# Pooled attention in an attention and two-MoE kernel: maxima scaled by ScalarE, a third batch's weights normalised there, and a re-planned order of issue

## The chip, the cores and the metric

The kernel runs on one core of a Trainium2 chip. The metric is the device time of one execution in microseconds (us). Before the change it is 820.82 us, the median of three runs (820.48 to 821.06).

## What is computed

Local and pooled attention over four batches, then two feed-forward layers in succession (2304 tokens, 512 to 2048 to 512), cut from the reference:

```python
q_d = q.reshape(B, H, Sd, factor, D).mean(axis=3)      # k_d and v_d likewise; factor 4
out_d = sm_attn(q_d, k_d, v_d)                          # softmax attention, 144 x 144 per head
out_up = np.repeat(out_d, factor, axis=2)
mask = np.abs(pos[:, None] - pos[None, :]) < factor
out_local = np.matmul(softmax(where(mask, scores, -1e9)), v)
x = (out_up + out_local)                                # B 4, H 8, S 576, D 64
h = x @ w_in;  g = np.maximum(0.01 * h, h);  x = g @ w_out          # layer 1
h = x @ w_in2; g = where(h >= 1, h, where(h <= -1, 0, (h + 1) ** 2 / 4)); out = g @ w_out2   # layer 2
```

## The kernel before

**A list of operations and a planner.** The kernel first makes a list of some thousands of operations (`Op`: an engine, a planned duration, the function that issues its instructions, the operations it depends on, a due time `key`). `Issue.run` then plays the list through in planned time: whenever an engine is free, the ready operation with the smallest rank on it is taken and its function called, so that its instructions stand next in the engine's queue. The order of every queue, and which buffer and PSUM bank an operation gets, come out of this. The numbers at the head of the file (due-time offsets per chain in `DUE`, leads, windows, latencies) steer it. The instructions' own semaphore waits are put in afterwards by the framework, from the data that they share.

**The operations of attention** stand in chains, one per pair of heads:

- `prep` loads q, k and v of batches 0 and 1 and transposes q and k on TensorE (L1185; its copies out of PSUM are ScalarE's, L1209).
- `down` is the pooled attention of one batch and head pair, four batches by four pairs. VectorE finds the row maxima (`peak`, L1367, two calls each for two heads by two row halves) and multiplies them by minus the softmax scale (L1368); ScalarE takes exponentials with that as bias (`pexp`, L1375); VectorE makes the reciprocal of the sums (L574, L575); then the weights are normalised (`norm`): by ScalarE in four calls where the batch is in `NORM_ACT_D` (L1388), otherwise by one VectorE multiplication (L1392).
- `local_p` and `local_d` are the local attention, on TensorE for batches 0 and 1 and most of it on VectorE for the rest (L1705 to L1779).

**Weights of the first layer** are converted to float32 by VectorE in three steps and split into two float16 parts, high by ScalarE and low by VectorE (first pairs: L701, L707, L713, L727, L729; in the second layer's stages L852 to L877). Every product of the two layers is three float16 matmuls.

**The layers.** Layer 1 is tiled into blocks of 512, 512, 512, 512 and 256 tokens: `g1` (L1934) makes a bank of hidden values by twelve matmuls, `g2` (L2196) multiplies it by the output weights. Layer 2 uses a seven-product scheme for both of its products: L1964 for the first, L2133 for the second, with the sums and splits in between on VectorE and ScalarE (L1995 to L2103). At a block's end its last sums go through `onto` (L2154) and a store (L2165).

**Fills.** Where the planner sees TensorE idle for want of work, up to the planned time `FILL`, it issues a matmul of zeros into a spare bank (`fill`, L2529). These stand in TensorE's queue like any other work.

The two functions of `down` that change read, before:

```python
nc.vector.reduce_max(ml(0, par), psv(par), axis=AX)               # peak, L1367
nc.vector.tensor_scalar_mul(ml(0, par), ml(0, par), -s_e)         # peak, L1368
...
nc.scalar.activation(out=p[:, par, a, :], in_=psv(par)[:, a, :], func=AF.Exp, scale=s_e,
                     bias=ml(0, par)[:, a:a + 1], accum_out=ml(1, par)[:, a:a + 1])   # pexp, L1375
```

Of the kernel before, what the change touches and what calls it, by code (L numbers as in the profile page):

```python
# [27 lines left out]
LEAD_O = 2  # L28
WINDOW_O = 15
OUT_GAP = 0.411  # L30
LAG7 = {0: 10, 1: 9, 2: 15, 3: 18, 4: 10}
G2LATE = {0: 7.366, 1: 6.364, 2: 4.968, 3: 5.548, 4: 9.226}
PASS2 = {0: 47.587, 1: 3.15, 2: 56.047, 3: 70.737, 4: 41.965}
SOON = 1000.0
FP = 2
T4_LATE = 12
EARLY_O = 4
W1_SPARE = 1957
LATE1 = 5.273
# [4 lines left out]
WINDOW_T = 7  # L44
# [5 lines left out]
WINDOW_A = 19  # L50
WINDOW_D = 15
LEAD_W = 6
LEAD_W1 = 1.5
LEAD_W1O = 1.477
RUSH_B = {1: 7.782}
RUSH_P = None
W1_RUSH = 0
QUEUE = 2.793
# [3 lines left out]
WINDOW_B = {2: 6, 3: 6}  # L62
LEAD_D = 2
# [4 lines left out]
DMA_END = 1.377  # L68
SW_END = 2.263
# [6 lines left out]
RUN_PE = 0.06  # L76
# [6 lines left out]
D_PE = 24.191  # L83
D_STRETCH = 1.006
W1_FROM = 9
W1_MORE = 1.467
# [10 lines left out]
PEAK_D = 4921  # L97
RESERVE = 3947
HP_GAP = 0.8
RESERVE_W = 0  # L100
SPARE = 5950

TWO_FROM = (2, 98)
WINDOW = 22
WINDOW_W = 34
LIMIT = 26744
AHEAD = 5
LEAD_Q = (12, 8)
O_LATE = 1.34
LAGMAX = 5  # L110
G2KEY = 1.87

NORM_ACT = (1,)
NORM_ACT_D = (1,)
FILL = 173.83


DUE = {0: -0.12, 2: 0.03, 3: -0.01, 9: 2.8, 10: -0.4, 14: -3.31, 17: -9.75, 19: -0.21,
# [129 lines left out]
class Issue:  # L248
# [4 lines left out]
    SHAPE = 0.093  # L253

# [36 lines left out]
    def run(self, fill=None):  # L291
# [16 lines left out]
        while left:  # L308
# [94 lines left out]
class Banks:  # L403
# [13 lines left out]
    def get(self, for_mlp=False):  # L417
        self.mlp += for_mlp
        self.begun |= for_mlp
        return self.free.pop(0)  # L420

# [6 lines left out]
def kernel(  # L428
# [85 lines left out]
    T_SC = 0.553  # L514
# [222 lines left out]
    class Pair:  # L737


        def __init__(self, n, nu):  # L740
# [3 lines left out]
            self.ready = []  # L744

# [382 lines left out]
    def prep(b, hp, due):  # L1128
# [93 lines left out]
        for nm in "qk":  # L1222
            c = None
            for i in range(2):
                n = (NA, QBB - NA)[i]
                t = ch.op("PE", pe_mm(RUN_PE * 2 * n, QB, 2 * n, D) if b in RUNS else pe_tr(QB, n, QB), lambda nm=nm, i=i: tr(nm, i), [ld[nm]], banks=1, shape=(1, 1) if b in RUNS else (2, 2),
# [12 lines left out]
    def down(b, hp, due):  # L1239
# [238 lines left out]
    def local_p(b, n0, cnt, hp, due):  # L1478
# [152 lines left out]
        x1[blk].ready.append(o)  # L1631
        ch.close()
# [10 lines left out]
    def local_d(u, due):  # L1643
# [201 lines left out]
        for par in range(2):  # L1845
# [16 lines left out]
            o = ch.op("DVE", 0.36 + 0.16 * sum((r == 0) + (r + n == SEGB) for _, n, _, r in rr),  # L1862
# [7 lines left out]
        for jh, j0 in enumerate(range(0, L, JC)):  # L1870
            last = []
            for par in (1, 0) if (0, j0) in v_act else (0, 1):
# [25 lines left out]
                ch.op("DVE", t_dve(512), lambda jh=jh: xl(jh), [h], after=freer(("x", jh))))  # L1898
        ch.close()
# [13 lines left out]
    def stage(m, b):  # L1913
# [8 lines left out]
        def g1(p, i):  # L1922
# [646 lines left out]
```

## Time and profile before

| | |
|---|---|
| median of the runs | 820.82 us |
| the profiled execution, its own time | 821.11 us |
| its span, first to last instruction | 819.3 us |
| TensorE busy | 812.0 us, 99%, 6791 matmuls |
| VectorE busy | 726.5 us, 89%, 1360 instructions |
| ScalarE busy | 499.1 us, 61%, 1283 instructions |
| granted TensorE clock, mean | 1.000 |

The profiled execution took 821.11 us, of which 1.81 us lie around its span. An engine's busy time is the time in which it had an instruction under way; matmuls overlap, so a busy TensorE may still be doing fills, or matmuls shorter than the time they are shown with. In the rows below PE is TensorE's matmuls, PEld its weight loads, DVE is VectorE, ACT ScalarE, POOL GpSimd and SP the queue that issues most transfers.

### The profile page before, as it was taken

The numbers are of one execution on the slowest core, as the hardware profiler recorded it, in microseconds if no ns is written. First come the engines' busy times: TensorE is split into PE (matmuls) and PEld (weight loads), VectorE is DVE, ScalarE is ACT, GpSimd is POOL, SyncE is SP. The second block draws the span as 40 slices with busy tenths as digits, with TensorE's granted clock in tenths as the row PEclk, the third lists the DMA queues.
The fourth block names the chain that finished last, engine by engine and source line by source line (L and its number), as shares of the span: only waits on it lengthen the run. The fifth ranks groups of instructions, "written<-read, shape, count | busy, mean of one in ns | idle before, by whom it ended". The sixth has DMA issues, their size and how long they took to land. (4 is left out here: it accounts for less than half of the span.)

```text
span 819.3 us, 17419 instructions
## 1 busy us (share of the span) xinstructions
PE 812.0 (99%) x6791; PEld 562.6 (69%) x6791; DVE 726.5 (89%) x1360; ACT 499.1 (61%) x1283; POOL 38.7 (5%) x60
## 2 busy tenths in 40 slices
PE   9999999999999999999999999999999999999997
PEld 6765554544454444544446888888888888889986
DVE  4999999999999999999999999999669697896761
ACT  4987667466436463473356677777567676775640
POOL 1010000033001310000000000000000000000000
PEclk9999999999999999999999999999999999999999
DMA  8877556576345822331733320010000200100001
GB/s 207 207 193 232 190 187 172 155 145 126 92 124 168 134 44 69 100 103 55 253 103 129 110 73 27 2 52 27 26 2 14 78 14 2 52 27 2 3 27 52
DMA packets 63521, 77.40 MB, mean 94 GB/s; under 512 B 17742, under 2 KB 41678, under 8 KB 63438
## 3 DMA queue, kind: packets, MB, share of 16 engines
q1 hardware_dynamic: 52238, 72.13, 28.4%
q0 software_dynamic: 11200, 4.15, 4.5%
q8 instruction: 53, 0.87, 0.4%
q14 instruction: 30, 0.25, 0.1%
HBM read 66.80 MB, written 9.44 MB: 93 GB/s over the span
## 5 line engine op out<-in xcount | busy, mean ns | idle before, releaser
L1934 PE MATMUL bank<-arena,w 128*128 128x512 f16 (+1 forms) x960 | 197.0, 358 | 0.0
L2196 PE MATMUL bank<-arena,w 128*128 128x512 f16 x768 | 176.4, 379 | 0.3 <-DVE arena L2176 0.3
L1934 PEld LDWEIGHTS <-w 128*128 128x128 f16 x960 | 92.5, 98 | 88.9 <-issue 1.9
L2196 PEld LDWEIGHTS <-w 128*128 128x128 f16 x960 | 92.0, 98 | 86.9 <-issue 2.3
L2133 PEld LDWEIGHTS <-w 128*128 128x128 f16 x1086 | 106.0, 98 | 12.2
L2133 PE MATMUL bank<-arena,w 128*128 128x256 f16 x810 | 96.8, 273 | 0.0
L1964 PEld LDWEIGHTS <-w 128*128 128x128 f16 x960 | 86.4, 98 | 10.0 <-issue 1.3
L2046 ACT ACTIVATE arena<-bank 128x512 f32<-128x512 f32 x64 | 38.0, 593 | 81.5 <-PE bank L1934 79.2
L2050 ACT ACTIVATE w<-bank,half 128x512 f32<-128x512 f32 x66 | 45.3, 687 | 41.5 <-DVE bank L2013 38.8
L1964 PEld LDWEIGHTS <-arena 128*128 128x128 f16 x720 | 64.8, 98 | 6.7
L2099 ACT ACTIVATE w<-w 128x256 f16<-128x256 f32 (+1 forms) x112 | 50.2, 478 | 17.4 <-DVE w L2058 13.2
L1964 PE MATMUL bank<-arena,w 128*128 128x256 f16 (+1 forms) x480 | 59.9, 267 | 0.6 <-DVE bank L2006 0.4
L2058 DVE SCALAR_TENSOR_TENSOR w<-w,bank 128x512 f32<-128x512 f32 x66 | 44.8, 681 | 15.0 <-ACT w L2054 14.0
L2103 DVE SCALAR_TENSOR_TENSOR w<-w 128x256 f16<-128x256 f32 (+1 forms) x112 | 53.1, 502 | 3.6 <-ACT w L2099 3.5
L1964 PE MATMUL bank<-w,w 128*128 128x256 f16 (+1 forms) x480 | 52.6, 256 | 0.0
L1995 ACT COPY w<-bank 128x256 f32<-128x256 f32 x106 | 36.4, 365 | 18.2 <-PE bank L1964 16.5
L2133 PEld LDWEIGHTS <-arena 128*128 128x128 f16 x426 | 41.6, 98 | 5.5 <-issue 0.7
L1964 PE MATMUL bank<-arena 128*128 128x256 f16 (+1 forms) x384 | 44.6, 266 | 0.0
L2176 DVE SCALAR_TENSOR_TENSOR arena<-arena 128x512 f16<-128x512 f32 x64 | 43.6, 682 | 0.3 <-ACT arena L2172 0.3
L1779 DVE TENSOR_TENSOR arena<-arena 128x768 f32<-128x768 f32 (+2 forms) x60 | 41.1, 687 | 1.4
L2054 ACT ACTIVATE w<-w 128x512 f32<-128x512 f32 x66 | 41.1, 628 | 1.2
L2172 ACT ACTIVATE arena<-arena 128x512 f16<-128x512 f32 x64 | 40.3, 630 | 0.9
(219 smaller groups left out, 1342.0 us busy)
## 6 DMA issues: line engine op xcount, KB each, us to landing
arena<-in_moe_w_in_dram SPq DMA_DIRECT2D x15, 1024.0 KB
arena<-in_moe_w_out_dram SPq DMA_DIRECT2D x8, 1024.0 KB
arena<-in_moe_w_out_dram SPq DMA_DIRECT2D x9, 512.0 KB
arena<-x SPq DMA_DIRECT2D x4, 1024.0 KB
x<-arena SPq DMA_DIRECT2D x15, 256.0 KB
w<-in_moe_w_out_dram SPq DMA_DIRECT2D x7, 512.0 KB
out_dram<-w SPq DMA_DIRECT2D x14, 256.0 KB
arena<-in_k_dram SPq DMA_DIRECT2D x23, 112.0 KB
```

The costliest lines, as they stand in the source:

```text
L1779: nc.vector.tensor_tensor(out, x, y, op=ALU.add)
L1934: nc.tensor.matmul(h[:, e], a[:, f // FP, c, f % FP], y[:, :, c, :], start=(n == 0), stop=(n == 3 * KDM - 1),)
L1964: nc.tensor.matmul(o[:, e], a[:, i, c], y[:, k, c, :], start=first and e == 0 and n == 0, stop=n == 5, skip_group_check=True,)
L2050: nc.scalar.activation(out=t, in_=st["h", p], func=AF.Relu, scale=0.5 * s_in, bias=half)
L2054: nc.scalar.activation(out=t, in_=t, func=AF.Square, scale=s_in ** -0.5)
L2058: nc.vector.scalar_tensor_tensor(out=t, in0=t, scalar=1.0 / s_in, in1=st["h", p], op0=ALU.min, op1=ALU.max)
L2099: nc.scalar.activation(out=left(p, part, q0, q1)[:, 0], in_=src(), func=AF.Copy, scale=so)
L2103: nc.vector.scalar_tensor_tensor(out=d[:, 1], in0=src(), scalar=so, in1=d[:, 0], op0=ALU.mult, op1=ALU.subtract)
L2133: nc.tensor.matmul(o[:, k], a[:, i, at:at + P], y[:, j], start=opens and p == e == k == n == 0, stop=p == PH - 1 and e == E - 1 and n == 2 ...
L2172: nc.scalar.activation(out=gv(p)[0], in_=st["t", p].ap, func=AF.Copy, scale=so)
L2176: nc.vector.scalar_tensor_tensor(out=lo, in0=st["t", p].ap, scalar=so, in1=hi, op0=ALU.mult, op1=ALU.subtract)
L2196: nc.tensor.matmul(o, a, y[:, e, :], start=(first and n == 0 and c % E == 0), stop=(last and n == 2), skip_group_check=True,)
```

## The change

- `peak` finds the negated maxima in one instruction; the multiplication by the scale moves from VectorE to ScalarE, at the head of `pexp`.
- `NORM_ACT_D` takes in batch 2, so that its pooled weights are normalised by ScalarE, four calls for each of four head pairs, in place of one VectorE multiplication each.
- The planner no longer adds an engine's hop (0.15 to 0.25 us of planned time) between two operations of the same engine.
- Many of the planner's numbers are others, among them `FILL`, `DUE`, `PASS2`, `G2LATE`, `LAG7` and several planned durations. Code for splitting the first `g1` by heads is added, but `EARLY = 0` leaves it unused.

```diff
-LAG7 = {0: 10, 1: 9, 2: 15, 3: 18, 4: 10}
-PASS2 = {0: 47.587, 1: 3.15, 2: 56.047, 3: 70.737, 4: 41.965}
+LAG7 = {0: 8, 1: 13, 2: 14, 3: 16, 4: 6}
+PASS2 = {0: 36.519231, 1: 8.162466, 2: 62.712205, 3: 115.505985, 4: 38.456233}
+EARLY = 0
...
-NORM_ACT_D = (1,)
-FILL = 173.83
+NORM_ACT_D = (1, 2)
+FILL = 60
...
-DUE = {0: -0.12, 2: 0.03, 3: -0.01, 9: 2.8, 10: -0.4, 14: -3.31, 17: -9.75, 19: -0.21,
...
+DUE = {0: -0.01, 2: -0.15, 4: 5.57, 5: -1.03, 6: -0.01, 7: -0.11, 9: 8.0, 10: -0.27, 12: -0.05,
...
-                    u.ready = max(u.ready, d + self.HOP[op.eng]
-                                  + (self.HOP_PE if u.eng == "PE" else 0.0))
+                    hop = 0.0 if u.eng == op.eng and not op.lat else (
+                        self.HOP[op.eng] + (self.HOP_PE if u.eng == "PE" else 0.0))
+                    u.ready = max(u.ready, d + hop)
...
-            nc.vector.reduce_max(ml(0, par), psv(par), axis=AX)
-            nc.vector.tensor_scalar_mul(ml(0, par), ml(0, par), -s_e)
+            nc.vector.reduce_max(ml(0, par), psv(par), axis=AX, negate=True)
...
             p = st["p"].ap[:GH].rearrange("p (h a g) -> p h a g", h=2, a=2)
+            nc.scalar.mul(ml(0, par), ml(0, par), s_e)
             for a in range(2):
                 nc.scalar.activation(
...
-            e = ch.op("DVE", 0.56, lambda par=par: peak(par), [o, e], need=() if par else (8,))
-            x = ch.op("ACT", 2 * t_act(G, True, 2), lambda par=par: pexp(par), [e, x],
+            e = ch.op("DVE", t_dve(2 * G), lambda par=par: peak(par), [o, e], need=() if par else (8,))
+            x = ch.op("ACT", 2 * t_act(G, True, 2) + 0.1, lambda par=par: pexp(par), [e, x],
```

What it makes of the queues is shown at three places. Lines of the changed kernel have other numbers: L1185 is there L1196, L1367 L1378, L1375 L1386, L1934 L1951, L2133 L2150, L2154 L2171, L2165 L2182 and L2529 L2554; its new L1384 is the scaling on ScalarE.

VectorE, early in batch 0's pooled attention, before:

```order
L1287 TENSOR_REDUCE w_61<-w_61 128x144
L1367 TENSOR_REDUCE w_61<-bank_69 72x2
L1368 TENSOR_SCALAR w_61<-w_61 72x2
L1278 TENSOR_TENSOR arena<-arena 72x4x128
L1280 TENSOR_TENSOR w_61<-arena 72x2x2x64
L1367 TENSOR_REDUCE w_61<-bank_64 72x2
L1368 TENSOR_SCALAR w_61<-w_61 72x2
```

ScalarE at the same chain, in the changed kernel:

```order
L1384 ACTIVATE w_61<-w_61 72x2
L1386 ACTIVATE arena,w_61<-bank_69,w_61 72x144 x2
L1568 COPY arena<-bank_65 70x512
L1384 ACTIVATE w_61<-w_61 72x2
L1386 ACTIVATE arena,w_61<-bank_70,w_61 72x144 x2
```

The 72x2 multiplications are gone from VectorE's queue and stand on ScalarE's, each right ahead of the two exponentials that use it; there are 32 of them.

TensorE just ahead of layer 1's first `g1`, before:

```order
L1512 MATMUL bank_66<-w_61,arena 64x70 x6
L1185 MATMUL bank_64<-ident,arena 64x64 x8
L2529 LDWEIGHTS zeros
L2529 MATMUL bank_63<-zeros 128x512
...
L1353 MATMUL bank_67<-w_61 72x144
L1353 MATMUL bank_69<-w_61 72x144
L1353 MATMUL bank_67<-w_61 72x144
L1353 MATMUL bank_69<-w_61 72x144
L1934 LDWEIGHTS w_79
L1934 MATMUL bank_68<-arena,w_79 128x512
```

and in the changed kernel:

```order
L1196 MATMUL bank_64<-ident,w_61 64x64 x10
L2554 LDWEIGHTS zeros
L2554 MATMUL bank_63<-zeros 128x512
L1564 MATMUL bank_65<-ident,w_61 70x128 x4
L1196 MATMUL bank_69<-ident,w_61 64x64 x8
L1196 MATMUL bank_68<-ident,w_61 64x64 x8
L1364 MATMUL bank_70<-w_61 72x144
...
L2554 LDWEIGHTS zeros
L2554 MATMUL bank_63<-zeros 128x512
L1951 LDWEIGHTS w_79
L1951 MATMUL bank_66<-arena,w_79 128x512
```

The real matmuls ahead of the first `g1` are the same but for batch 1's transposes (L1185, 216 before, 252 now). Of the fills 40 stood ahead of it and 11 behind; now 43 stand ahead and none behind. What the first `g1` needs of VectorE is its first 144 instructions before and 141 now: eight L1368 less, and more by one local maximum (L1525) and the four instructions of a third weight tile of 128x512 (L701 to L729). Of ScalarE it needs 121 before and 136 now, eight of the new ones being L1384.

VectorE at the program's end, before:

```order
L2154 SCALAR_TENSOR_TENSOR w_79<-bank_67,w_79 128x256
L2154 SCALAR_TENSOR_TENSOR w_79<-bank_63,w_79 128x256
L2154 SCALAR_TENSOR_TENSOR w_79<-bank_64,w_79 128x512
L2154 SCALAR_TENSOR_TENSOR w_79<-bank_70,w_79 128x512
```

and in the changed kernel:

```order
L2171 SCALAR_TENSOR_TENSOR w_79<-bank_67,w_79 128x256
L2171 SCALAR_TENSOR_TENSOR w_79<-bank_65,w_79 128x512
L2171 SCALAR_TENSOR_TENSOR w_79<-bank_63,w_79 128x256
L2171 SCALAR_TENSOR_TENSOR w_79<-bank_67,w_79 128x256
```

The last sum and the store behind it are now those of the block of 256 tokens, half as wide (128x256, 128 KB in place of 256 KB).

## Rows read from the trace of the kernel before

**Rows 1.** The page, busy time, share of the span, instructions.
```profile
PE 812.0 (99%) x6791; PEld 562.6 (69%) x6791; DVE 726.5 (89%) x1360; ACT 499.1 (61%) x1283; POOL 38.7 (5%) x60
```

**Rows 2.** The page, granted TensorE clock in 40 slices, tenths of full speed.
```profile
PEclk9999999999999999999999999999999999999999
```

**Rows 3.** Four stages by windows: us, busy us (instructions) by engine, clock, DMA share, GB/s.
```profile
0.00:20.00 20.00, 18.80 (x288) 11.93 (x290) 9.69 (x32) 9.39 (x34) 3.81 (x22) 1.00 0.80 206
20.00:58.00 38.00, 38.00 (x662) 28.55 (x660) 35.48 (x116) 33.64 (x149) 4.24 (x7) 1.00 0.79 207
58.00:120.00 62.00, 62.00 (x544) 33.14 (x543) 60.17 (x116) 45.45 (x143) 1.58 (x5) 1.00 0.65 205
120.00:440.00 320.00, 319.62 (x1741) 154.48 (x1739) 314.98 (x470) 166.47 (x454) 29.03 (x26) 1.00 0.46 122
```

**Rows 4.** The chain that ended last, last part: start, us, what.
```profile
798.28 0.43 DVE w L2154
...
798.75 15.89 PE bank L2133 x144
...
814.67 0.69 DVE w L2154
```

**Rows 5.** Windows of L2529 alone (fills): us, PE busy (count), PEld busy (count).
```profile
0.00:58.00 58.00, 15.43 (x40) 3.86 (x40) 1.00 0.80 207
58.00:120.00 62.00, 3.41 (x11) 0.91 (x11) 1.00 0.65 205
```

**Rows 6.** PE's waits from 58 us on: us in total, times, longest.
```profile
PE bank L2133 <- DVE w L2154: 0.5, 1, 0.5
PE bank L1964 <- DVE bank L2006: 0.4, 1, 0.4
PE bank L2196 <- DVE arena L2176: 0.3, 1, 0.3
PE bank L1964 <- DVE bank L2013: 0.2, 1, 0.2
```

**Rows 7.** Groups by line: count, busy us, mean ns, idle before.
```profile
L1368 DVE TENSOR_SCALAR w<-w 72x2 f32<-72x2 f32 x16 | 2.7, 166 | 0.6
...
L1392 DVE TENSOR_TENSOR arena<-arena 72x576 f32<-72x576 f32 x8 | 6.0, 748 | 0.0
...
L1388 ACT ACTIVATE w<-w 72x144 f32<-72x144 f32 x8 | 2.7, 408 | 1.7 <-DVE w L575 1.7
...
L1864 ACT ACTIVATE arena<-arena 128x56 f32<-128x56 f32 x10 | 2.5, 251 | 10.8 <-DVE arena L1734 10.8
...
L1375 ACT ACTIVATION_READ_ACCUMULATOR arena<-bank,arena 72x1 f32 x32 | 6.3, 197 | 0.0
```

**Rows 8.** Windows of L1368 alone: us, DVE busy (count).
```profile
0.00:120.00 120.00, 1.99 (x12) 1.00 0.72 206
```

**Rows 9.** Timeline, 0 to 14 us: start, us, engine, line, what.
```profile
1.20 4.02 PE L2529 MATMUL bank<-zeros 128*128 128x512 bf16 x9 [1.20 <-DVE half L533]
...
7.16 1.73 PE L1185 MATMUL bank<-ident,w 64*64 64x64 f32 x52
```

**Rows 10.** Timeline, around 93 us.
```profile
91.08 0.68 DVE L713 SCALAR_TENSOR_TENSOR w<-arena,w 128x512 int32<-128x512 int32 x1
...
92.02 1.22 DVE L729 SCALAR_TENSOR_TENSOR w<-arena,w 128x1024 f16<-128x1024 f32 x1
...
93.30 0.82 PE L2529 MATMUL bank<-zeros 128*128 128x512 bf16 x3
...
93.96 0.81 PE L1934 MATMUL bank<-arena,w 128*128 128x512 f16 x3
```

**Rows 11.** Timeline, the end.
```profile
802.88 0.42 DVE L2154 SCALAR_TENSOR_TENSOR w<-bank,w 128x256 f32<-128x256 f32 x1 [4.18 <-PE bank L2133]
...
815.39 0.38 SPq L2165 DMA_DIRECT2D out_dram<-w  x1
```

More of the change, by code (lines that the diff above doesn't have):

```diff
@@ L27 @@
 OUT7 = (0,1,2,3,4)
-LEAD_O = 2
-WINDOW_O = 15
-OUT_GAP = 0.411
-LAG7 = {0: 10, 1: 9, 2: 15, 3: 18, 4: 10}
-G2LATE = {0: 7.366, 1: 6.364, 2: 4.968, 3: 5.548, 4: 9.226}
-PASS2 = {0: 47.587, 1: 3.15, 2: 56.047, 3: 70.737, 4: 41.965}
+LEAD_O = 5
+WINDOW_O = 30
+OUT_GAP = 0.369438
+LAG7 = {0: 8, 1: 13, 2: 14, 3: 16, 4: 6}
+G2LATE = {0: 12.156149, 1: 14.308722, 2: 2.469313, 3: 8.213399, 4: 16.039018}
+PASS2 = {0: 36.519231, 1: 8.162466, 2: 62.712205, 3: 115.505985, 4: 38.456233}
 SOON = 1000.0
 FP = 2
-T4_LATE = 12
+EARLY = 0
+EARLY_ROOM = 0
+T4_LATE = 8.301867
 EARLY_O = 4
-W1_SPARE = 1957
-LATE1 = 5.273
+W1_SPARE = 3131
+LATE1 = 8.859782
 LEAD_S = 4
@@ L43 @@
 LEAD_T = 4
-WINDOW_T = 7
+WINDOW_T = 8
 LEAD = 5
@@ L49 @@
 RUSH = 1.0e4
-WINDOW_A = 19
-WINDOW_D = 15
+WINDOW_A = 17
+WINDOW_D = 22
 LEAD_W = 6
-LEAD_W1 = 1.5
-LEAD_W1O = 1.477
-RUSH_B = {1: 7.782}
+LEAD_W1 = 1.06903
+LEAD_W1O = 2.28811
+RUSH_B = {1: 7.935746}
 RUSH_P = None
 W1_RUSH = 0
-QUEUE = 2.793
+QUEUE = 2.381903
 WHOLE = ()
@@ L61 @@
 POOLED = ()
-WINDOW_B = {2: 6, 3: 6}
-LEAD_D = 2
+WINDOW_B = {2: 7, 3: 6}
+LEAD_D = 1
 D_GAP = 4
@@ L67 @@
 DMA_LAST = 0.85
-DMA_END = 1.377
-SW_END = 2.263
+DMA_END = 1.710062
+SW_END = 0.8
 SW_FIRST = 1.88
@@ L82 @@
 LAT_W = (1.95, 1.95)
[L83 to L86, printed above, removed]
+D_PE = 80
+D_STRETCH = 0.871542
+W1_FROM = 10
+W1_MORE = 1.749148
 D_ACT = (0,1)
@@ L96 @@
 ADD_PE = ()
-PEAK_D = 4921
-RESERVE = 3947
-HP_GAP = 0.8
+PEAK_D = 5347
+RESERVE = 2527
+HP_GAP = 0.695866
 RESERVE_W = 0
-SPARE = 5950
+SPARE = 5857
 TWO_FROM = (2, 98)
[L104 to L111, printed above, removed]
-NORM_ACT = (1,)
-NORM_ACT_D = (1,)
-FILL = 173.83
-DUE = {0: -0.12, 2: 0.03, 3: -0.01, 9: 2.8, 10: -0.4, 14: -3.31, 17: -9.75, 19: -0.21,
[7 rows of a table removed]
+WINDOW = 24
+WINDOW_W = 29
+LIMIT = 26359
+AHEAD = 4
+LEAD_Q = (10, 8)
+O_LATE = 4.133946
+LAGMAX = 7
+G2KEY = 1.232175
+NORM_ACT = (1,)
+NORM_ACT_D = (1, 2)
+FILL = 60
+DUE = {0: -0.01, 2: -0.15, 4: 5.57, 5: -1.03, 6: -0.01, 7: -0.11, 9: 8.0, 10: -0.27, 12: -0.05,
[9 rows of a table added]
 class Arena:
@@ L420, in get, with hold @@
         return self.free.pop(0)
+    def hold(self):
+        self.mlp += 1
+        return self.get()
     def put(self, t, for_mlp=False):
@@ L744, in __init__ @@
             self.ready = []
+            self.by = {c: [] for c in range(KDM)}
         def make(self):
@@ L1861, in local_d @@
                 reds.append(o)
-            o = ch.op("DVE", 0.36 + 0.16 * sum((r == 0) + (r + n == SEGB) for _, n, _, r in rr),
+            o = ch.op("DVE", 0.36 + 0.32 * sum((r == 0) + (r + n == SEGB) for _, n, _, r in rr),
                       lambda par=par: soft1(par), reds, need=(L,))
@@ L1898, in local_d @@
                 ch.op("DVE", t_dve(512), lambda jh=jh: xl(jh), [h], after=freer(("x", jh))))
+            for by in x1[blk].by.values():
+                by.append(ch.ops[-1])
         ch.close()
@@ L1920, in stage, with g1 @@
         x = x1[b] if m == 1 else None
-        def g1(p, i):
-            sch.step = max(sch.step, i)
-            h_open[0] += 1
+        def g1(p, i, cs=range(KDM)):
+            if KDM - 1 in cs:
+                sch.step = max(sch.step, i)
+                banks.begun = True
             hi, lo = x[0], x[1]
             whi, wlo = w_in[m]
-            st["h", p] = banks.get(True)
+            if 0 in cs:
+                h_open[0] += 1
+                st["h", p] = banks.hold()
             h = st["h", p].rearrange("p (a u n) -> p a u n", a=E, n=x.nu)
@@ L1930, in g1 @@
                 f = E * p + e
-                n = 0
-                for c in range(KDM):
+                n = 3 * cs[0]
+                for c in cs:
                     for a, y in ((whi, hi), (whi, lo), (wlo, hi)):
@@ L2269, in stage @@
             fs = [E * p + e for e in range(E)]
-            o1 = sch.add(
+            o1 = None
+            if m == 1 and not b and p < EARLY:
+                for c in range(KDM):
+                    o1 = sch.add(
+                        "PE", 3 * t_mm(N) * E, lambda p=p, i=i, c=c: g1(p, i, (c,)),
+                        x.by[c] + [o1] + [w_ready[m, 0, f] for f in fs], key=float(i),
+                        banks=0 if c else 1, mlp=True, cols=3 * 512,
+                        gate=None if c else (lambda: len(banks.free) > EARLY_ROOM))
+            o1 = o1 or sch.add(
                 "PE", 12 * t_mm(N) * E, lambda p=p, i=i: g1(p, i),
```

8 lines of the change are left out of this document (5 added, 3 removed), and 16 rows, old and new, of the table DUE.

## The prediction

> **What bounds the kernel now.** I read the page's busy times first. TensorE is busy for 99% of the span and VectorE for 89% [rows 1]. Both cannot be the bound everywhere, so I then read the same by stages [rows 3]. Up to 20 us every engine waits for the first loads and for the others. From 20 to 440 us VectorE works almost without a break: 35.48 of 38 us, 60.17 of 62, 314.98 of 320. TensorE shows as full there too, but part of what it does is multiplying zeros: 40 fills with 15.43 us of busy time up to 58 us, where the first `g1` starts, and 11 with 3.41 us between 58 and 120 us [rows 5]. Behind 120 us there are no fills, and TensorE's waits on VectorE from 58 us to the end come to four, 1.4 us in all [rows 6]. The chain that ended last shows the rest: TensorE, broken by VectorE for 0.43 us at 798 us, and a last VectorE sum of 0.69 us [rows 4].
>
> So TensorE's real work is the floor, and this change takes none of it away. What can be won is the time in which TensorE has no real work: the fills, the 1.4 us of waits, and the 4.6 us behind its last matmul. Everything behind 58 us comes to 3.4 + 1.4 us and a piece of the tail. That caps the gain however much VectorE is relieved.
>
> **The change, part by part.**
>
> *VectorE's relief.* 32 multiplications by the scale go, at 0.166 us [rows 7]: 5.3 us. Four of the normalisations go (batch 2, one for each head pair), at 0.748 us [rows 7]: 3.0 us. Together 8.3 us of 726.5. The negated maximum takes the place of the plain one, same shape, and I cost that at nothing. All of this lies in the stages that VectorE fills, yet only 12 of the scalings, 2.0 us, fall before 120 us [rows 8], and the normalisations of batch 2 come later. Behind 120 us there are only waits to win. So 6.3 of the 8.3 us meet a TensorE that hardly waits.
>
> *ScalarE's load.* 32 scalings of 72x2: the trace has none. The nearest rows are 0.197 us (reading an accumulator, one element) and 0.251 us (56 elements) [rows 7]. I take 0.25, as that is an activation too: 8.0 us, 6.3 at the lower price. Sixteen normalising calls at 0.408 us [rows 7] add 6.5 us. Together 14.5 us on an engine with 62.0 - 45.45 = 16.6 us idle from 58 to 120 us and 153.5 from 120 to 440 [rows 3]. What hides it there is that idle time. From 20 to 58 us it has only 38.0 - 33.64 = 4.4 us, and each scaling stands ahead of two exponentials, with other chains' copies behind them. There the cover may be gone, so I price it in the next term.
>
> *Up to the first `g1`.* By the orders shown, it needs three instructions less of VectorE. Eight scalings go, 1.3 us, but five come, at 0.68 us or less (the 128x512 conversion [rows 10]): 3.4 us at most, so up to +2.1 us. Of ScalarE it needs 15 more of the kind that fills this stage: 33.64 / 149 = 0.23 us each [rows 3], +3.4 us. Ahead of it TensorE does 36 more of batch 1's transposes, which count twice in the trace: 72 x 1.73 / 52 = 2.4 us [rows 9]. This is work taken from behind. If VectorE decides, the term is 2.1 - 2.4 = -0.3 us; if ScalarE does, 3.4 - 2.4 = +1.0. If the idle time of both swallows the extra work, it is -2.4; if ScalarE decides and the transposes only fill its waits, +3.4. I take **+0.4**, halfway between the two engines, because both are over 88% busy there.
>
> *From 58 to 120 us.* The 11 fills lie where a `g1` or a part of attention was late. VectorE, the engine that they wait for most (the low halves of the weights, L729, are its last step), now has 2.0 us less ahead. The fills also cost something by themselves: at 93 us the low half was done at 92.02 + 1.22 = 93.24 us, but three fills stood next in the queue from 93.30, and the `g1` began at 93.96 [rows 10]. In the new order none stands behind the first `g1`. I take **-2.0**, VectorE's relief; the ends are 0, when the waits stay as waits, and -3.4, when all fills were idle time that goes.
>
> *From 120 us to the last pass.* Of the 1.4 us of waits, 0.5 is that of L2133 on L2154 near the end [rows 6]. The order still has this pair, a sum that reads a bank between two groups of matmuls into it, so it stays. The other 0.9 are short lags behind VectorE, which now comes with 8.3 us less done. I take **-0.6**, with 0 and -0.9 as ends, since part of each lag is the way from one engine to the next, which no relief shortens.
>
> *The end.* The last sum is of 128x256 in place of 128x512: 0.42 for 0.69 us [rows 4, 11]. The store behind it is half as large; the one before took from 815.39 us to the end of the span at 819.3, 3.9 us [rows 11], and what part goes with size no row tells. I take -0.1, with 0 and -1.95 as ends. Together **-0.4**.
>
> *The planner's hop* moves planned times, not waits: the instructions keep their semaphores. Its effect is the order, counted above. In a row of two dependent small operations VectorE stands idle 0.6 us for 16 of them [rows 7], so packing these costs little.
>
> **Sum:** +0.4 - 2.0 - 0.6 - 0.4 = -2.6 us on the profiled execution's 821.11, 818.5. That execution is 0.3 us above the median of 820.82, so against the median I expect **818.2 us**. With the ends of the four terms this forecast reaches from about 816.6 to 819.8. A measurement of this kernel can tell about 0.2%, 1.6 us, from no change: below 819.2 is faster, above 822.5 slower.
>
> **The rivals.**
>
> *All of it goes* (faster still). The idle time takes the extra start work (-2.4), all fills and lags go (-3.4, -0.9), the end gives -0.4: -7.1, **813.7 us**. For it speaks that the new planner saw no need for a fill behind the first `g1`. Against it, VectorE still has 97% of its time filled, and relief of 2.0 us does not end 3.4 us of lateness.
>
> *The waits only change their name* (no change). TensorE waits without fills where it had them, because VectorE is last by as much as before: +0.4, 0, -0.6, -0.4, **820.2 us**. For it speaks VectorE's 97% from 58 to 120 us [rows 3] and that three of its instructions for a weight tile weigh more than all eight scalings gone up to the first `g1`.
>
> *ScalarE ends last* (slower). Up to the first `g1` it has 3.4 us more and 4.4 us idle. If less than 3.4 of those can be filled, because an exponential waits for a maximum while copies queue behind it, the `g1` starts up to 3.4 us later, the transposes win nothing, and the stage to 120 us keeps its lateness: +3.4 + 0 - 0.6 - 0.4 = +2.4, **823.2 us**. For it speaks ScalarE's 33.64 of 38 us; against it, 16.6 us of room right behind.
>
> *TensorE's clock falls* (slower). The first nine fills took 4.02 us, 0.43 us each [rows 9]: 512 columns at the lower of the two levels, 1.2 GHz, though the clock row shows full speed in every slice [rows 2]. After those, three fills took 0.66 us from the first's start to the `g1` [rows 10], 0.22 each, which is 2.4 GHz. Between 58 and 120 us waits were covered by fills; now they are bare. If the clock drops twice, at nine matmuls x 0.21 us = 1.9 us each, and the fills' time stays: +0.4 + 3.8 - 0.6 - 0.4 = +3.2, **824.0 us**. By the Trainium skill ("TensorE: Matmul & The Clock Gate", the section on the HAM clock gate), the array's clock is held at half until activity releases it, and falls back after idleness; by that rule, taking fills away where TensorE lacks work is a risk. The trace shows the release at the start; at 798 us it shows a bare wait of 0.5 us [rows 6] behind which 144 matmuls took 15.89 us [rows 4], 0.11 us for 256 columns, full speed. So short waits are safe, and I give this little.
>
> **How the numbers follow.** Chances: the forecast 0.45, all of it goes 0.12, waits that change their name 0.25, ScalarE last 0.13, the clock 0.05. The forecast's own range lies below 819.2 for all but 0.05; the no-change case gives 0.04 to faster, 0.20 to same and 0.01 to slower; of ScalarE's case, 0.04 lies under 822.5. So faster 0.40 + 0.12 + 0.04 = 0.56, same 0.05 + 0.20 + 0.04 = 0.29, slower 0.01 + 0.09 + 0.05 = 0.15. The range of 814.6 to 822.8 us takes in the forecast, the no-change case, and about half of what lies beyond on either side.
>
> **What would show it.** Right: the first `g1` between 57 and 61 us; between it and 120 us TensorE's idle time (waits, no fills) under 1.5 us; VectorE's busy time down by about 8 us, ScalarE's up by about 14; the wait before a 256-column pass near the end still there, and a last sum of 0.42 us. Wrong: a first `g1` beyond 62 us with ScalarE over 95% busy from 20 us on; TensorE waits of more than 3 us from 58 to 120 us; 512-column matmuls that follow each other at 0.43 us behind the start; or new waits of TensorE behind 440 us, where I count on none.

## The result, and the profile after

The changed kernel takes **828.06 us** (median of 5 runs, 826.63 to 828.39) against 820.56 us for the kernel before in the same comparison: **1.0083** times, 95% interval 1.0070 to 1.0097. The forecast was 818.2 us and the range ended at 822.8, so it missed in sign and size. The profiled execution took 826.63 us, the shortest of the five; 824.8 of it are its span, 5.5 us more than before.

The page's busy times of the changed kernel, which answer to [rows 1]:

```profile
PE 810.9 (98%) x6783; PEld 561.3 (68%) x6783; DVE 726.2 (88%) x1324; ACT 515.0 (62%) x1331; POOL 38.5 (5%) x60
```

VectorE has 36 instructions less, as counted in the forecast, and its busy time has not moved: 726.2 us for 726.5. ScalarE has 15.9 us more, close to the 14.5 that I added up.

The stages of the changed kernel by windows (as [rows 3]; the last two stages are new):

```profile
20.00:58.00 38.00, 37.85 (x673) 28.46 (x671) 36.90 (x114) 34.07 (x154) 4.19 (x9) 1.00 0.82 197
58.00:120.00 62.00, 62.00 (x520) 33.37 (x516) 59.47 (x112) 50.09 (x168) 1.45 (x3) 1.00 0.62 197
120.00:440.00 320.00, 318.10 (x1733) 153.30 (x1733) 313.82 (x442) 174.73 (x469) 28.93 (x26) 1.00 0.47 125
440.00:540.00 100.00, 95.23 (x857) 83.66 (x856) 97.92 (x171) 70.75 (x136) 0.00 (x0) 1.00 0.20 70
...
540.00:812.00 272.00, 270.60 (x2635) 243.29 (x2633) 206.13 (x454) 174.43 (x369) 0.00 (x0) 1.00 0.07 22
```

And the kernel before in those last two:

```profile
440.00:540.00 100.00, 99.42 (x896) 87.37 (x895) 99.51 (x178) 74.22 (x144) 0.00 (x0) 1.00 0.17 59
540.00:812.00 272.00, 271.49 (x2651) 245.00 (x2649) 205.96 (x452) 169.89 (x365) 0.00 (x0) 1.00 0.08 28
```

From 440 to 540 us TensorE was idle for 4.77 us where it had been for 0.58, while VectorE was busy for 98 of the 100 us. Ahead of that, from 120 to 440 us, its idle time rose from 0.38 to 1.90 us. TensorE's waits behind 58 us (as [rows 6]: in total, times, longest):

```profile
PE bank L1981 <- DVE bank L2023: 3.9, 5, 1.4
PE bank L1981 <- ACT w L2012: 1.6, 1, 1.6
PE bank L1413 <- ACT arena L2189: 1.2, 1, 1.2
PE bank L2150 <- DVE w L2171: 0.5, 1, 0.5
```

L1981 (L1964 before) is a product of the seven-product scheme, and its operands are sums and halves that VectorE makes. The wait of 1.6 us bears ScalarE's name; the chain that ended last shows what it was (start, us, what):

```profile
466.04 1.14 DVE w L888
467.17 0.61 DVE w L863
467.79 0.02 issue
467.81 1.24 DVE w L869
469.04 0.02 issue
469.07 1.23 DVE w L875
470.30 0.02 issue
470.32 0.62 ACT w L885
470.94 0.34 issue
471.29 0.36 ACT w L2012
471.65 0.04 issue
471.69 0.83 PE bank L1981 x6
```

ScalarE's copy stood behind another of its operations, and that one waited for VectorE, which had no break. So VectorE is what TensorE waits for behind 440 us, in a kernel that gave VectorE less work than before.

**Where VectorE's time went.** The timeline of the changed kernel on VectorE (start, us, line, what):

```profile
467.09 0.68 DVE L863 TENSOR_SCALAR w<-arena 128x1024 int32<-128x1024 int32 x1
467.81 1.22 DVE L869 SCALAR_TENSOR_TENSOR w<-arena,w 128x1024 int32<-128x1024 int32 x1
469.07 1.22 DVE L875 SCALAR_TENSOR_TENSOR w<-arena,w 128x1024 int32<-128x1024 int32 x1
```

and the same three steps in the kernel before (L852, L858; the third follows later):

```profile
463.05 0.68 DVE L852 TENSOR_SCALAR w<-arena 128x1024 int32<-128x1024 int32 x1
463.65 0.68 DVE L1063 TENSOR_TENSOR arena<-arena 128x512 f32<-128x512 f32 x1
464.26 1.21 DVE L858 SCALAR_TENSOR_TENSOR w<-arena,w 128x1024 int32<-128x1024 int32 x1
465.39 0.68 DVE L1063 TENSOR_TENSOR arena<-arena 128x512 f32<-128x512 f32 x1
```

Before, steps of other work stand between, and each row starts 0.07 to 0.08 us *before* the one ahead has ended (463.65 against 463.05 + 0.68). After, each step needs the one ahead of it, and starts 0.04 us *behind* its end (467.81 against 467.77). I took this for all of VectorE's instructions from their starts and ends in the traces and from the semaphores that they wait for: an instruction that waits for none but the one directly ahead starts 34 ns behind its end (median of 195 before and of 253 after); one that waits for nobody starts 81 ns ahead of it. The difference is 0.115 us. One that waits for VectorE's own instruction two places back starts 81 ns ahead too (median of 125 before; 83 ns, of 77, after), so one instruction of other work between is enough. I call an instruction that waits for the one directly ahead a *dependent neighbour*. Counting those too that wait for another engine as well, VectorE has **222 of them before and 300 after**, ScalarE 76 and 173 (ScalarE's medians are 32 ns behind and 94 ahead). The planner without its hop within an engine sees no reason to put other work between.

### The profile page after: what moved, and what is told of

Read it like the earlier page. It is cut to its first block, busy times and chain, and to the rows that moved or that the text cites. A ratio compares the mean times of both kernels' runs of the same rounds, so it can differ in the third digit from the quotient of the medians.

```text
span 824.8 us, 17384 instructions
## 1 busy us (share of the span) xinstructions
PE 810.9 (98%) x6783; PEld 561.3 (68%) x6783; DVE 726.2 (88%) x1324; ACT 515.0 (62%) x1331; POOL 38.5 (5%) x60
## 4 chain that ended last, share of the span: by engine, by line
DVE 46%; PE 41%; ACT 6%; issue 4%; DMA 2%; SPq 1%; DVEq 0%; ACTq 0%
PE bank L2150 13%; PE bank L1981 9%; PE bank L1951 7%; PE bank L2213 6%; DVE arena L1717 4%; DVE arena L1725 4%; DVE arena L1791 3%; DVE arena L2193 3%; DVE arena L1761 2%; DVE w L2075 2%; DVE arena L869 2%; DVE w L2120 2%; DVE arena L888 2%; DVE arena L875 2%; DVE arena L972 2%
## 5 line engine op out<-in xcount | busy, mean ns | idle before, releaser
L1951 PE MATMUL bank<-arena,w 128*128 128x512 f16 (+1 forms) x960 | 197.3, 358 | 0.0
L1951 PEld LDWEIGHTS <-w 128*128 128x128 f16 x960 | 92.5, 98 | 88.5 <-issue 1.6
L2213 PEld LDWEIGHTS <-w 128*128 128x128 f16 x960 | 92.5, 98 | 88.5 <-issue 2.5
L1981 PEld LDWEIGHTS <-w 128*128 128x128 f16 x960 | 86.5, 98 | 15.3 <-issue 6.4
L2150 PEld LDWEIGHTS <-w 128*128 128x128 f16 x888 | 86.7, 98 | 10.6 <-issue 0.7
L1981 PE MATMUL bank<-arena,w 128*128 128x256 f16 (+1 forms) x672 | 81.9, 265 | 4.5 <-DVE bank L2023 3.9
L1981 PEld LDWEIGHTS <-arena 128*128 128x128 f16 x720 | 64.8, 98 | 8.6 <-issue 2.0
L2150 PEld LDWEIGHTS <-arena 128*128 128x128 f16 x624 | 60.8, 98 | 7.0
L1981 PE MATMUL bank<-arena 128*128 128x256 f16 (+1 forms) x528 | 62.6, 268 | 1.6 <-ACT w L2012 1.6
L2150 PE MATMUL bank<-arena,w 128*128 128x256 f16 x468 | 56.8, 273 | 0.0
L2116 ACT ACTIVATE w<-w 128x256 f16<-128x256 f32 (+1 forms) x101 | 45.9, 477 | 17.0 <-DVE w L2075 12.1
L2150 PE MATMUL bank<-arena 128*128 128x256 f16 x450 | 54.0, 273 | 0.0
L2150 PE MATMUL bank<-w 128*128 128x256 f16 x420 | 51.6, 273 | 0.5 <-DVE w L2171 0.5
L2120 DVE SCALAR_TENSOR_TENSOR w<-w 128x256 f16<-128x256 f32 (+1 forms) x101 | 48.2, 503 | 0.6 <-ACT w L2116 0.2
L2071 ACT ACTIVATE w<-w 128x512 f32<-128x512 f32 x70 | 43.9, 629 | 2.2
```

Source lines behind the costliest of these rows:

```text
L1951: nc.tensor.matmul(h[:, e], a[:, f // FP, c, f % FP], y[:, :, c, :], start=(n == 0), stop=(n == 3 * KDM - 1),)
L1981: nc.tensor.matmul(o[:, e], a[:, i, c], y[:, k, c, :], start=first and e == 0 and n == 0, stop=n == 5, skip_group_check=True,)
L2071: nc.scalar.activation(out=t, in_=t, func=AF.Square, scale=s_in ** -0.5)
L2116: nc.scalar.activation(out=left(p, part, q0, q1)[:, 0], in_=src(), func=AF.Copy, scale=so)
L2120: nc.vector.scalar_tensor_tensor(out=d[:, 1], in0=src(), scalar=so, in1=d[:, 0], op0=ALU.mult, op1=ALU.subtract)
L2150: nc.tensor.matmul(o[:, k], a[:, i, at:at + P], y[:, j], start=opens and p == e == k == n == 0, stop=p == PH - 1 and e == E - 1 and n == 2 ...
```

## The experiments

The theories: **T1**, dependent neighbours give VectorE's relief back; **T2**, ScalarE's added work in the attention chains is what costs; **T3**, the planner's new numbers make a worse order; **T5**, the numbers fit one order and any other loses; **T6**, the moves win nothing, only the order does.

**1. The hop put back or taken away, one at a time.** In the changed kernel:

```diff
-                    hop = 0.0 if u.eng == op.eng and not op.lat else (
-                        self.HOP[op.eng] + (self.HOP_PE if u.eng == "PE" else 0.0))
-                    u.ready = max(u.ready, d + hop)
+                    u.ready = max(u.ready, d + self.HOP[op.eng]
+                                  + (self.HOP_PE if u.eng == "PE" else 0.0))
```

> The changed kernel with only the planner's hop between operations of one engine put back (0.15 us on VectorE, 0.2 us on ScalarE); ScalarE's scalings, the third batch's normalising by ScalarE and all new numbers of the planner stay. Dependent neighbours: VectorE 193 (300 in the changed kernel), ScalarE 99 (173). T1: 107 x 0.116 = 12 us less on VectorE, busy near 714 us, and 9 us less on ScalarE; the kernel at 815 to 822 us. T2: ScalarE's added work stays, so 826 to 830 us. T3: the numbers stay, so 826 to 832 us.

Measured: 833.97 us, 1.0160 (1.0146 to 1.0174), outside every theory's range. VectorE's busy time fell from 726.2 to 719.4 us, in T1's direction but by 7 us for 12, and the kernel didn't follow. Numbers found for one rule and used under another draw a bad order. The same edit the other way in the kernel before:

> The kernel before with only the planner's hop between operations of one engine taken away; VectorE keeps the scalings, the numbers of the planner are those of before. Dependent neighbours: VectorE 329 (222 before), ScalarE 140 (76). T1: 107 x 0.116 = 12 us more on VectorE, busy near 738 us, the kernel at 828 to 836 us. T2: no work moved to ScalarE, so 820 to 822 us. T3: the numbers are the old ones, so 820 to 823 us.

Measured: 844.40 us, 1.0290 (1.0275 to 1.0304); VectorE's busy time rose from 726.5 to 735.9 us. The sign is T1's, the size is 8 us beyond it. With both moves to ScalarE on top:

> The kernel before with the scalings and the third batch's normalising moved to ScalarE and the planner's hop within an engine taken away, but with all the planner's numbers of before. Dependent neighbours: VectorE 297, ScalarE 171, as in the changed kernel. T1: 8 us of work less and 75 pairs x 0.116 = 8.7 us more on VectorE, busy near 727 us; the kernel at 824 to 830 us. T2: all of ScalarE's added work is there, 826 to 830 us. T3: with the old numbers the loss goes, 818 to 822 us.

Measured: 834.10 us, 1.0162 (1.0148 to 1.0176). Against T3: the old numbers lose more than the new ones. T1's range ended at 830 us, 4 us short of it. In all three the whole order was drawn anew, so none of them prices a neighbour. That took experiments in which the order stays.

**2. Neighbours made dependent, the order unchanged.** After the program is written, in the kernel before (EXTRA is a list of positions on VectorE):

```diff
         consts()
         sch.run(fill)
+        dve = [i for i in nc.cur_bb.bb.instructions if i.engine == mybir.EngineType.DVE]
...
+        for k in EXTRA:
+            tc.add_manual_dep(dve[k], dve[k - 1].name, mybir.DependencyInfo(
+                mybir.DependencyClass.Sync, mybir.DependencyReason.DATA), reason="neighbour")
```

> The kernel before, its instructions and their order unchanged on every engine; 80 instructions of VectorE between 58 and 520 us, spread evenly over those that waited for nobody, wait in addition for the one directly ahead of them. Dependent neighbours on VectorE 302 (222 before), as many as in the changed kernel (300). T1 (a dependent neighbour costs VectorE 0.116 us and the kernel with it): VectorE's 1360 instructions end 80 x 0.116 = 9.3 us later by 520 us, the kernel at 826 to 831 us. T2 and T3 (ScalarE's added work, the planner's new numbers): neither is here, 820.3 to 822 us.

> As the run with 80, but 161 such waits between 58 and 520 us, 383 dependent neighbours. T1: 161 x 0.116 = 18.7 us of VectorE's time, the kernel at 834 to 840 us, twice the loss of the run with 80. T2 and T3: 820.3 to 822 us.

Measured: **828.71 us** with 80, 1.0096 (1.0082 to 1.0110), and **839.17 us** with 161, 1.0225 (1.0211 to 1.0239), against 821.04: +7.7 and +18.1 us, 0.096 and 0.113 us of kernel for each. Nothing else differs, so this is shown: a wait for the instruction directly ahead, with the same work in the same order, costs this kernel about 0.1 us. That 80 of them cost what the changed kernel lost is no account of that kernel yet, as its VectorE also has less work. TensorE's clock doesn't explain it: in both profiled executions the granted clock was 0.98 from 440 to 540 us, but of the runs with 161 waits the one at a mean clock of 0.996 took 838.19 us and the one at 0.998 took 840.18. The pages' busy times, 80 first:

```profile
PE 814.0 (98%) x6791; PEld 563.0 (68%) x6791; DVE 733.2 (89%) x1360; ACT 498.6 (60%) x1283; POOL 38.6 (5%) x60
```

```profile
PE 816.0 (98%) x6791; PEld 563.0 (67%) x6791; DVE 740.3 (89%) x1360; ACT 499.0 (60%) x1283; POOL 38.5 (5%) x60
```

726.5, 733.2, 740.3: 0.084 and 0.086 us of busy time for each (an overlap of 81 ns that is gone), and the 34 ns beside it are idle. One of the 80, in the timeline of that run (L863 is the L858 shown above):

```profile
469.16 0.68 DVE L1068 TENSOR_TENSOR arena<-arena 128x512 f32<-128x512 f32 x1
469.87 1.23 DVE L863 SCALAR_TENSOR_TENSOR w<-arena,w 128x1024 int32<-128x1024 int32 x1
```

It starts 0.03 us behind the row ahead, where it had started 0.07 us ahead of its end. TensorE's waits behind 58 us with 161:

```profile
PE bank L1974 <- DVE w L1066: 4.1, 1, 4.1
PE bank L2206 <- DVE arena L2186: 3.4, 4, 1.3
PE bank L1974 <- DVE bank L2016: 2.0, 3, 0.8
```

The same for ScalarE:

> The kernel before, instructions and order unchanged; 97 instructions of ScalarE between 58 and 820 us that waited for nobody wait in addition for the one directly ahead of them. Dependent neighbours on ScalarE 173 (76 before), as many as in the changed kernel. T1 for both engines: ScalarE 97 x 0.126 = 12 us slower, the kernel 3 to 8 us slower, 824 to 829 us. T1 for VectorE alone (ScalarE has idle time of 40%): 820.5 to 822.5 us.

Measured: 823.11 us, 1.0027 (1.0015 to 1.0038), +2.0 us. Below the range of T1 for both engines and a little above that of T1 for VectorE alone: ScalarE's idle time takes most of it.

**3. A control for the order.** VectorE's hop at 0.14 in the place of 0.15:

> A control: the kernel before with VectorE's hop to itself at 0.14 us in the place of 0.15, so the planner draws another order with as many dependent neighbours (VectorE 221, ScalarE 64; before 222 and 76). T1: only what another order costs by chance, 818 to 828 us. Theory T5 (the planner's numbers fit one order, and any other order loses as much as the run without the hop did, 24 us): 835 to 845 us.

Measured: 825.17 us, 1.0051 (1.0038 to 1.0063). An order drawn anew costs 4.1 us by itself; T5 falls for the 24 us of experiment 1, but no run that draws a new order can be read to better than some 4 us. Nor does the place of the loss tell its cause: with 221 neighbours this order leaves TensorE idle in the same stretch as the changed kernel, for 5.23 us:

```profile
440.00:540.00 100.00, 94.77 (x848) 82.74 (x847) 98.24 (x173) 70.70 (x137) 0.00 (x0) 1.00 0.24 80
```

**4. The moves alone, in the old planner and in the old order.**

> The kernel before with both moves to ScalarE (the scalings and the third batch's normalising), with the hop within an engine kept (0.14 us on VectorE, 0.2 us on ScalarE) and with the planner's old numbers. Dependent neighbours: VectorE 201, ScalarE 104. T1: VectorE loses 8 us of work and 2 us of pairs, busy near 717 us; the kernel at 812 to 822 us, and what the control shows of another order on top. T2 (ScalarE's work costs the time): 826 to 832 us. T5: 830 us or more.

Measured: 824.61 us, 1.0044 (1.0032 to 1.0057), VectorE busy 721.6 us. Beside the control that is no gain; T1's range ended at 822 us without what another order costs. So I made the moves with every other instruction in its place:

```diff
-            nc.vector.reduce_max(ml(0, par), psv(par), axis=AX)
-            nc.vector.tensor_scalar_mul(ml(0, par), ml(0, par), -s_e)
+            nc.vector.reduce_max(ml(0, par), psv(par), axis=AX, negate=True)
...
+            nc.scalar.mul(ml(0, par), ml(0, par), s_e)
             for a in range(2):
...
-            if b in NORM_ACT_D:
+            if b in (1, 2):
```

> The kernel before with only the scalings of the pooled maxima moved to ScalarE (32 small multiplications leave VectorE), the planner told nothing of it, so that every other instruction keeps its place on its engine. Dependent neighbours on VectorE 190 (222 before). T1 (VectorE's time is what the kernel follows, at the rate that the runs with 80 and 161 added waits showed, 0.10 us of kernel for each): VectorE about 5 us less, the kernel at 815 to 819 us. T2 (ScalarE's added work in the attention chains costs the time): 6 us more of ScalarE, 822 to 828 us.

> As the run with the scalings alone, and the third batch's pooled weights normalised by ScalarE too, again with every other instruction in its place. T1: another 4 x 0.75 = 3 us off VectorE, the kernel at 812 to 818 us. T2: 823 to 830 us.

Measured: 820.89 us for the scalings, 1.0003 (0.9994 to 1.0011), and 822.10 us for both, 1.0018 (1.0008 to 1.0028). T1's reading of these runs, that relief pays back at the rate at which waits cost, is wrong, and both runs lie below T2's ranges too. VectorE's busy time fell to 723.0 and 721.0 us, and what it won it waited away. VectorE's longest sums of waits from 58 to 520 us, both moves made (in total, times, longest):

```profile
DVE arena L2176 <- ACT arena L2172: 4.5, 7, 1.6
DVE arena L574 <- ACT arena L1375: 1.3, 2, 1.0
```

The first of these was 0.3 us before. ScalarE in turn waits for TensorE, as it did before (L2046, the step ahead of L2172, for L1934: 79.3 us in 43 waits). TensorE's queue, fills included, is fixed in these runs and was idle for only 1.4 us behind 58 us [rows 6], so a relief of VectorE can win hardly more than that, while a burden makes TensorE wait. Whether ScalarE's added work took a part of the relief as well was not tested. In the changed kernel TensorE does wait for VectorE; there I put the scalings back:

> The changed kernel with the scalings put back on VectorE, the planner told nothing of it, so that every other instruction keeps its place. T1: VectorE 5 us more, the kernel at 830 to 835 us. T2: ScalarE 6 us less in the chains, 820 to 825 us.

Measured: 832.79 us, 1.0148 (1.0135 to 1.0162), 4.7 us above the changed kernel's 828.06. There VectorE is the bound, and the move of the scalings to ScalarE is worth 5 us. T2 falls.

**5. The hop put back late.** From 430 us of the plan on, in the changed kernel:

```diff
-                    hop = 0.0 if u.eng == op.eng and not op.lat else (
+                    hop = (0.0 if t < 430 else {"DVE": 0.15, "ACT": 0.2, "PE": 0.27}.get(u.eng, 0.14)) \
+                        if u.eng == op.eng and not op.lat else (
```

> The changed kernel with the hop within an engine put back from 430 us of the planner's time on; up to there (about 440 us of the chip's) the order is that of the changed kernel to the instruction. Dependent neighbours on VectorE 259 (300 in the changed kernel), ScalarE 136 (173). T1: TensorE stands at 440 us as in the changed kernel, and of its 9 us of waits behind that, 3 to 7 go: 820 to 824 us, up to 826 us if the order drawn anew costs as much as in the control with 0.14 us. T2 and T3: 826 to 830 us.

Measured: 827.37 us, 1.0080 (1.0066 to 1.0094). VectorE's dependent neighbours from 440 to 520 us fell from 22 to 4, and TensorE's idle time from 440 to 540 us stayed, 3.97 us for 4.77:

```profile
440.00:540.00 100.00, 96.03 (x850) 83.73 (x848) 96.39 (x168) 69.37 (x132) 0.00 (x0) 0.98 0.18 63
```

T1's range is missed, and the time lies in that of T2 and T3. So the neighbours of that stretch are not the cause, or not the only one, of the waits that show there. They may come from neighbours on the way (208 up to 440 us, for 165 before), or from the order, which was drawn anew here from 430 us on as in the control; this run does not part the two.

**6. A swap at the last moment.** The changed kernel's order, but an operation of VectorE that needs the one ahead lets the next one pass:

```diff
...
+                        if held is None and last in best.deps and not best.need \
+                                and not best.banks:
+                            held = best
+                        else:
+                            self.emit(best)
+                            last = best
+                            if held is not None:
+                                held.fn()
+                                last, held = held, None
...
```

> The changed kernel with its planned order and its instructions kept; only in the writing-out of VectorE's stream, an operation that depends on the one directly ahead of it lets the next operation pass, where that one depends on neither. Neighbours on VectorE that depend on each other: 245, against 300 in the changed kernel and 222 before. Theory T1 (a dependent neighbour costs VectorE 0.116 us more, and the planner now makes 78 more of them): 55 fewer pairs x 0.116 = 6.4 us of VectorE's time come back, VectorE busy near 720 us, kernel 820 to 824 us. Theory T2 (the added work and hops of ScalarE in the attention chains hold TensorE): ScalarE is untouched, 827 to 829 us. Theory T3 (the new planner numbers make a worse order): the order is the same but for neighbours, 827 to 829 us.

Measured: 846.27 us, 1.0307 (1.0286 to 1.0327). A miss for every theory. VectorE's busy time fell only to 725.2 us, and it now waits. VectorE's longest sums of waits from 58 to 520 us in this run (the changed kernel's largest there is 1.1 us):

```profile
DVE arena L2216 <- ACT arena L2212: 10.6, 11, 2.3
DVE arena L607 <- ACT arena L1409: 3.4, 3, 1.1
```

The operations let past waited for ScalarE and held up what they had passed. TensorE's clock seems to add to it: its mean lay between 0.989 and 0.996 in these executions (0.999 to 1.000 in those of the changed kernel), and the one at 0.996 was the shortest, 842.85 us. So the run says nothing about the price of a neighbour. To part neighbours, the work put between must be ready on the chip, not only in the plan.

**7. Both moves, the hop kept, new numbers.** The planner of before with both moves and its hop, and its numbers (due times, windows, leads) searched anew for the earliest end of its own plan:

```diff
-LAG7 = {0: 10, 1: 9, 2: 15, 3: 18, 4: 10}
...
+LAG7 = {0: 10, 1: 11, 2: 17, 3: 18, 4: 10}
...
-WINDOW_B = {2: 6, 3: 6}
+WINDOW_B = {2: 4, 3: 7}
...
-NORM_ACT_D = (1,)
+NORM_ACT_D = (1, 2)
...
```

> Both moves to ScalarE, the hop within an engine kept as before, the planner's numbers found anew for this rule; the planner ends its own plan at 808.7 us (before 812.5, changed kernel 810.5). Dependent neighbours: VectorE 190, ScalarE 106. Theory T1 (plans that know what a neighbour costs are kept by the chip: their spans came 0.5 to 7 us above the plan, those of plans without the hop 14 to 20 us): span 809 to 816 us, the kernel at 811 to 817 us. T2 (ScalarE's added work costs the time): 822 us or more. T5 (the old order alone is good): 824 us or more, as in the two runs that drew it anew with the old hop.

> As the run a, with other numbers; the plan ends at 809.8 us. Dependent neighbours: VectorE 192, ScalarE 102. T1: span 810 to 817 us, the kernel at 812 to 818 us. T2: 822 us or more. T5: 824 us or more.

Measured: **817.45 us**, 0.9962 (0.9949 to 0.9976), and **817.93 us**, 0.9967 (0.9955 to 0.9980); spans 814.8 and 815.8. T1's ranges hold but for run a's time, 0.45 us above its own; T2 and T5 fall. The moves are no loss; run a beats both kernels. Its page and TensorE's waits behind 58 us:

```profile
PE 805.5 (99%) x6770; PEld 561.4 (69%) x6782; DVE 718.8 (88%) x1324; ACT 509.4 (63%) x1331; POOL 38.6 (5%) x60
```

```profile
PE bank L2133 <- DVE w L2154: 0.5, 1, 0.5
PE bank L1964 <- DVE bank L2013: 0.2, 1, 0.2
PE bank L1353 <- ACT arena L1341: 0.2, 1, 0.2
```

VectorE's busy time is now 7.7 us lower, the relief that the changed kernel should have had, with 190 dependent neighbours.

Whether that gain is the moves' or the search's, two runs tell. In run a's order, both pieces of work back on VectorE (the edits of experiment 4 the other way round):

> Run a with both pieces of work put back on VectorE, the planner told nothing of it, every other instruction in its place. Dependent neighbours on VectorE 222. T1 (VectorE has no slack in an order that was drawn for the moves): 8 us of work and 32 neighbours come back, the kernel 4 to 9 us above run a, 821 to 827 us. T6 (the moves win nothing, the new order does): 817 to 819 us.

Measured: 824.51 us, 1.0041 (1.0027 to 1.0055), 7.1 us above run a. And the same search without the moves:

> The kernel before, no moves to ScalarE, the hop kept, with the planner's numbers searched anew as for run a and for as long; the plan ends at 811.05 us (before 812.5, run a 808.7). Dependent neighbours: VectorE 215, ScalarE 67. T1 with the moves as the source of run a's gain: span 813 to 819 us and the kernel 819 to 821 us, above run a. T6: as good as run a, 816 to 818.5 us.

Measured: 820.15 us, 0.9992 (0.9983 to 1.0001), no change from before. T6 falls by the first of the two: undoing the moves costs 7 us in an order drawn for them, and making them wins nothing in the order before. The second run agrees, but as a new order it is read to 4 us only, and it lies 2.7 us above run a. Against the kernel before, moves and search together win 3.6 us.

**Plan and chip.** While the program sets its order it plans a time for each operation, and so an end. Set against the measured spans these plans fall into two groups (us; the plan's end is no measurement):

| kernel | plan | span | over |
|---|---|---|---|
| hop kept: before | 812.5 | 819.3 | 6.8 |
| hop 0.14 | 817.1 | 822.6 | 5.5 |
| both moves, old numbers | 820.8 | 822.8 | 2.0 |
| changed kernel with the hop | 831.6 | 832.0 | 0.4 |
| run a | 808.7 | 814.8 | 6.1 |
| run b | 809.8 | 815.8 | 6.0 |
| no moves, new numbers | 811.05 | 818.1 | 7.1 |
| no hop: changed kernel | 810.5 | 824.8 | 14.3 |
| before without the hop | 823.5 | 843.3 | 19.8 |
| before, moves, without the hop | 814.7 | 832.5 | 17.8 |

The changed kernel's plan ends 2 us ahead of the one before, so its numbers and moves do win by its own account. But that account holds dependent neighbours for free, and 300 of them aren't. With the hop as it was, the plan charges 0.15 us for what measured 0.115, and the chip keeps it to within about 7 us.

## Why the prediction was wrong, step by step

*Up to the first `g1`*: +0.4 forecast, and right. It starts at 60.74 us, 2.7 us later, of which 2.4 are the transposes taken from behind. *ScalarE ends last* falls with it: ScalarE was busy for 34.07 of the 38 us, and the stage behind did not keep its lateness.

```profile
60.52 0.39 PE L2554 MATMUL bank<-zeros 128*128 128x512 bf16 x1
60.74 1.46 PE L1951 MATMUL bank<-arena,w 128*128 128x512 f16 x6
```

*From 58 to 120 us*: -2.0 forecast, between 0 and -3.4. Behind the first `g1` no fill begins, for eleven before [rows 5]; the last one begins at 60.52 us, ahead of it. Their absence from the order was no sign that TensorE would have work, as *All of it goes* took it: `FILL = 60` forbids fills behind 60 us of the plan. That TensorE shows no idle time there (62.00 of 62.00 us above) is the sign. Counted by the real matmuls begun, each at the time between two starts that its kind takes in the kernel before, the changed kernel stands 2.6 us ahead at 120 us. These two terms had promised 1.6.

*The end*: -0.4 forecast. From the end of the last matmul to the end of the span 4.0 us (820.79 to 824.8) for 4.7, and the wait of 0.5 us before the last pass is still there. Right. *TensorE's clock* was granted in full in every stage above, so that rival falls for the changed kernel.

*From 120 us to the last pass*: -0.6 forecast, and this is the term that failed. TensorE's shown idle time alone grew by 1.5 us from 120 to 440 us, 4.2 to 540 and 0.9 to 812: **+6.6**. A matmul of 256 columns is shown with 0.27 us, but the next starts 0.11 us behind it, so a pause is shown some 0.16 us too short. By the matmuls begun, the changed kernel is still 0.9 us ahead at 440 us and 3.7 behind at 540; its last matmul ends 6.2 us later (820.79 for 814.63). From 2.6 ahead that makes **+8.8** for this term, and with -2.6 and -0.7 for the others the 5.5 us by which the spans differ. Of the signs that the forecast had named, the new waits behind 440 us came, and the fall of VectorE's busy time by about 8 us did not.

The step behind it is *"The planner's hop moves planned times, not waits ... so packing these costs little"*. Two things were wrong in it. First, the waits are where the instructions stand: the semaphores stayed, but next to its source each one became a real wait. Second, I priced a dependent neighbour by the idle time in its row, 0.6 us for 16 [rows 7], 0.038 us. That is the 34 ns behind its predecessor, right in itself and a third of the price. The other 81 ns are an overlap that independent instructions have and that a busy time, which counts overlapping instructions once, hides. The sum had nothing for them. By the starts and ends in the two traces, the 234 neighbours up to 540 us (172 before) take 7.6 us more of VectorE's time, nearly the 8.3 us that the moves were to give back. That 78 neighbours by the 0.096 us of the run with 80 make just the 7.5 us by which the medians differ is in part luck: it leaves the relief out, and in the changed order that was worth 5 us for the scalings alone. I had the order of both kernels, and could have counted them.

*VectorE's relief* of 8.3 us was right as a number of work removed (run a's VectorE has 7.7 us less) and would have been spent as I said, on a TensorE that hardly waits: in the order before it is worth nothing (experiment 4). That run's 822.10 us lies near the 820.2 of the rival *the waits only change their name*, but with the fills still in place, so it is no test of that rival's mechanism. *All of it goes*, 813.7 us, was reached by no run; run a came nearest. What I didn't have as a rival was VectorE falling back to where TensorE waits for it, with less work to do. The forecast's own range of 816.6 to 819.8 was too narrow for its terms, whose ends (-0.3 and +1.0 for the first) add up to 814.0 and 821.5; the measured time lies beyond both.

Open: of the changed kernel's loss, how much is neighbours and how much the order that its numbers give was not parted. The price of a neighbour is shown in the order before (experiment 2); in the changed order the swap (experiment 6) brought waits of its own, and the late hop (experiment 5) drew a new order. The control moved this kernel by 4 us with no more neighbours.

## What to carry to other kernels

Between operations of one engine the distance to the operation needed counts, not only its being there: put independent work between (here one instruction was enough), but only work that is ready on the chip. Before crediting relief on an engine, see which engine the kernel follows: the moves to ScalarE were worth nothing in one order, 5 us (the scalings alone) in another and 7 us in a third. A planner that sets an order must charge for a dependence within an engine, and its plan is to be set against a measured span before its end is believed.

## What the runs showed of the hardware

On VectorE an instruction that waits for the one directly ahead starts 34 ns behind its end, 104 ns when it also waits for another engine; one that needn't wait, or waits for an instruction two places back, starts 81 ns ahead of it. 80 such waits in an unchanged order cost 7.7 us, 161 cost 18.1. The Trainium skill ("VectorE: DVE Perf Modes", "The DRAIN you can't avoid") says of eight chained copies that a semaphore after each costs nothing extra, and (in "Rules for kernel authors") that one should lessen the count of operations and not the semaphores. The runs here differ, by 0.096 to 0.113 us for each wait, and the measurement decides.

On ScalarE the medians are 32 ns behind and 94 ns ahead; 97 more dependent neighbours there cost the kernel 2.0 us only, with 39% of ScalarE's time idle. The Trainium skill ("ScalarE: Activation LUTs", "What ACT_TABLE_LOAD costs") gives an overlap of about 93 ns between consecutive ACTIVATEs, which agrees; that it goes when one needs the other is what the traces add.
